# Channel-mix weights: f64 words loaded into their parts' room and converted there, 3 of 17 blocks in stage 1

## The chip, the cores and the metric

One NeuronCore of a Trainium2 chip runs the whole kernel. The metric is device time in microseconds (us) of one execution. The engines are called TensorE (PE in the profile, PEld for its weight loads), VectorE (DVE), ScalarE (ACT), GpSimd (POOL) and SyncE (SP, which here only issues DMAs).

## What is computed

Batch 4, 768 tokens, width 384. Three layers follow one another.

```python
# A: RWKV-like recurrence, 8 heads of 48
y[t] = r[t] @ (state + (u*k[t]) v[t]);  state = w[t]*state + k[t] v[t]
# B: 4 single-head causal attentions of width 64, each token gated to 2 of them
a = softmax(scale * (x wq[e]) (x wk[e])^T);  x = sum of gate * (a (x wv[e]) wo[e])
# C: channel mix, x_prev is x one token earlier
xk = mu_k*x + (1-mu_k)*x_prev;  xr = mu_r*x + (1-mu_r)*x_prev
out = sigmoid(xr @ w_r) * (maximum(xk @ w_k, 0)**2 @ w_v)
```

`w_k` (384x1024), `w_v` (1024x384) and `w_r` (384x384) of C arrive as float64, all else as float32. The products of B and C go through float32r in two parts: a number is a rounded high part and the rest, the low part, and three matmuls (high by high, low by high, high by low) stand for one.

## The kernel before

**Stages.** Stage 1 runs A for all batches, with B woven in as a second stream, and a third stream for the f64 conversion. It ends when A has ended: the pool `pA`, which holds A's tiles, is closed at line 1055. Stage 2 (lines 1068 to 1086) runs the rest of B with C for the first three batches, which goes over nine units of 256 tokens (`c_thin`, line 936). The end (`c_wide`, line 964) is C for the last batch in two units of 384 tokens.

**Order.** `run_all` (line 88) takes the next piece from the stream with the least progress, so the text order of A, B and C is fixed by costs written into the streams. A piece that yields nothing is put aside until another stream has moved. A scheduler of the language then orders each engine's instructions by that order and by its own model of when operands are ready.

**A, per pair of heads** (`a_prep`, `a_kt`, `a_u`, `a_pair`, 16 pairs): transposes, two long scans (lines 220 and 246) and products on VectorE, small matmuls on TensorE, a masking on GpSimd (line 338). Loads of the next pair go through SyncE's queue.

**B, per batch** (`phase_b`, line 575): values, gating, two projections of q and k (`proj`, line 544), 24 score blocks with a softmax, transposes (`trans`), products with the values (`av`) and with `wo` (`wo_half`, which stores x2 to DRAM through ScalarE's queue). In `trans` the transposed block goes from PSUM to SBUF on ScalarE (line 694), or on VectorE (line 692) for the blocks that `AT_DVE` (batches below `AT_B`) or `AT_DVE2` names; these are all 512 columns wide. In `proj` k's high part is written by ScalarE for one half of the partitions (line 142) and copied to the other half by a DMA of SyncE's queue (line 571).

**The conversion** (`c_convert`, `split_block`, lines 788 to 826): 34 blocks, 12 of `ck` (256 columns), 6 of `cr` and 16 of `cv` (192 columns), 7296 columns in all. Each is loaded through SyncE's queue into `c_raw` (two buffers). ScalarE scales the upper word (line 802), VectorE does three integer operations (803 to 805), ScalarE rounds to the high part (807), GpSimd subtracts for the low part (808), and two DMAs store both to DRAM. The integer operations use c_w1, written c_w in the rows.

**The weights in stage 2** (`c_weights`, line 828): six loads of GpSimd's queue bring both parts from DRAM into the pool `pW`, which lies where `pA` was, so the first waits for the end of A.

**C, per unit**: `c_load` brings x2 with one token ahead; `c_mix` forms xk (index 0) and xr (index 1); `c_hidden` makes eight blocks of 128 hidden columns (m = 0 to 7), `c_out` the gate `pz` from `cr` and the output `pvo` from `cv`. Within `c_hidden` the mix of xr goes along as a side stream, in `c_out` the next unit's mix of xk.

## Time and profile before

| what | value |
|---|---|
| median of 3 runs | 726.49 us (726.14 to 726.61) |
| profiled execution, its own time | 727.12 us |
| its span in the trace | 725.4 us |
| PE busy, share of the span | 672.8 us, 93% |
| PEld busy | 585.4 us, 81% |
| DVE busy | 497.9 us, 69% |
| ACT busy | 409.2 us, 56% |
| POOL busy | 299.7 us, 41% |
| moved by DMA | 77.88 MB |

Busy shares are means over the stages. Stage 1 lasts to about 325 us, stage 2 to about 640 us, the end to 725 us. The conversion's instructions stand between 66 and 248 us. A matmul's end is modelled, so busy PE is not PE at its peak. The profiled execution lies 1.7 us over its span and 0.6 us over the median of the runs.

### The profile page before, as it was taken

How to read it: one execution, taken by the hardware profiler on the slowest of the kernel's cores; microseconds unless marked ns; L12 is line 12 of the kernel's file. 1: busy time of each engine (PE TensorE's matmuls, PEld its weight loads, DVE VectorE, ACT ScalarE, POOL GpSimd, SP SyncE). 2: the span in 40 equal slices, each digit the busy share in tenths (PEclk: the TensorE clock that was granted, in tenths of full speed). 3: DMA queues.
4: the chain of work that ended last, by engine and by line, in shares of the span. 5: the costliest groups of instructions: out<-in, count | busy, mean ns of one | idle time of the engine just before them, and what ended most of it. 6: DMA issues, size and time to landing. Idle time of an engine off the chain costs nothing.

```text
span 725.4 us, 13681 instructions
## 1 busy us (share of the span) xinstructions
PE 672.8 (93%) x4938; PEld 585.4 (81%) x4938; DVE 497.9 (69%) x938; ACT 409.2 (56%) x1117; POOL 299.7 (41%) x397
## 2 busy tenths in 40 slices
PE   5887978889799999997999999999999999999995
PEld 4776856676577786866999899889898888989995
DVE  8988899998999888754543756556457573729520
ACT  3554556666576566656735657465556656534530
POOL 5876444343445222204625435362343515352320
PEclk9999899999999999999999999999999999999999
DMA  8797666668677653159320103211101101220001
GB/s 157 152 184 173 176 180 175 170 174 251 148 198 186 170 126 83 33 187 411 100 67 11 45 12 99 98 34 44 55 34 44 23 13 34 86 68 23 12 23 38
DMA packets 144205, 77.88 MB, mean 107 GB/s; under 512 B 109824, under 2 KB 138752, under 8 KB 143616
## 3 DMA queue, kind: packets, MB, share of 16 engines
q1 hardware_dynamic: 139936, 64.73, 35.1%
q0 software_dynamic: 864, 7.47, 2.6%
q10 hardware_dynamic: 3328, 4.72, 1.8%
q8 instruction: 41, 0.67, 0.4%
q14 instruction: 36, 0.29, 0.1%
HBM read 47.40 MB, written 23.99 MB: 98 GB/s over the span
## 4 chain that ended last, share of the span: by engine, by line
PE 64%; DVE 18%; DMA 8%; issue 4%; ACT 3%; POOL 1%; SPq 1%; ACTq 0%; DVEq 0%; POOLq 0%
PE ph L871 14%; PE pvo L871 14%; PE pz L871 5%; PE pa L710 5%; PE pq L518 4%; PE pt L681 3%; PE po L518 3%; PE py L368 3%; PE pv L518 3%; DMA c_raw<-in_moe_w_v_dram 2%; DVE ex L246 2%; PE psc L624 2%; PE pg L329 2%; DVE suf L220 2%; DVE rt L255 2%
## 5 line engine op out<-in xcount | busy, mean ns | idle before, releaser
L633 DVE TENSOR_REDUCE st<-psc 128x1 f32<-128x384 f32 (+4 forms) x128 | 62.1, 499 | 56.4 <-PE psc L629 41.3
L891 POOL TENSOR_TENSOR rl<-rl 128x256 f32<-128x256 f32 (+1 forms) x88 | 59.3, 678 | 78.5 <-ACT rl L890 78.3
L865 POOL TENSOR_TENSOR ml<-m,mh 128x256 fp32r<-128x256 f32 x54 | 40.6, 751 | 108.5 <-ACT mh L864 97.4
L645 ACT ACTIVATE A<-psc,st 128x384 f32<-128x384 f32 (+4 forms) x128 | 68.8, 542 | 20.2 <-DVE st L642 13.3
L871 PE MATMUL ph<-mh,ckh 128*128 128x256 f32 (+1 forms) x264 | 78.8, 299 | 0.9 <-ACT m L858 0.8
L871 PE MATMUL ph<-mh,ckl 128*128 128x256 f32 (+1 forms) x264 | 76.9, 292 | 1.5 <-DMA ckl<-ck_l_scratch 1.5
L338 POOL TENSOR_SCALAR_AFFINE_SELECT at<-at 128x512 f32<-128x512 f32 x48 | 44.7, 932 | 79.2 <-ACT at L337 79.0
L871 PE MATMUL ph<-ml,ckh 128*128 128x256 f32 (+1 forms) x264 | 76.9, 294 | 0.0
L871 PE MATMUL pvo<-cvh,hh 128*128 128x384 f32 x192 | 65.5, 341 | 0.0
L329 PE MATMUL pg<-rt,kt 128*128 128x256 f32 x192 | 53.8, 407 | 12.3 <-DVE um L307 5.8
L894 POOL TENSOR_TENSOR hl<-rl,hh 128x256 fp32r<-128x256 f32 x72 | 53.8, 756 | 27.0 <-ACT hh L892 26.7
L871 PE MATMUL pvo<-cvl,hh 128*128 128x384 f32 x192 | 64.6, 336 | 0.0
L871 PE MATMUL pvo<-cvh,hl 128*128 128x384 f32 x192 | 64.0, 336 | 0.0
L681 PE MATMUL pt<-ident,A 128*128 128x128 f32 x336 | 57.7, 275 | 0.0
L624 PE MATMUL psc<-k,q 128*128 128x384 f32 (+4 forms) x128 | 49.0, 383 | 9.0 <-ACT A L645 6.2
L890 ACT ACTIVATE rl<-ph 128x256 f32<-128x256 f32 (+1 forms) x88 | 35.5, 405 | 37.6 <-PE ph L871 26.2
L871 PEld LDWEIGHTS ph<-mh,ckh 128*128 128x128 f32 x264 | 49.9, 189 | 3.3 <-ACT m L858 1.0
L710 PE MATMUL pa<-at,vs 128*64 128x384 f32 (+2 forms) x288 | 52.1, 425 | 0.5 <-ACT at L694 0.5
L871 PEld LDWEIGHTS ph<-mh,ckl 128*128 128x128 f32 x264 | 50.0, 190 | 1.8 <-DMA ckl<-ck_l_scratch 1.8
L871 PEld LDWEIGHTS ph<-ml,ckh 128*128 128x128 f32 x264 | 49.9, 190 | 1.5 <-issue 1.5
L329 PEld LDWEIGHTS pg<-rt,kt 128*128 128x128 f32 x192 | 34.4, 197 | 19.8 <-DVE um L307 6.8
L861 DVE SCALAR_TENSOR_TENSOR m<-x2c,mu,m 128x256 f32<-128x256 f32 (+1 forms) x66 | 35.2, 539 | 20.4 <-ACT m L858 15.8
(172 smaller groups left out, 1917.3 us busy)
## 6 DMA issues: line engine op xcount, KB each, us to landing
x_scratch<-xs SPq DMA_DIRECT2D x24, 288.0 KB, 4.0
x<-x_scratch SPq DMA_DIRECT2D x6, 1152.0 KB, 8.4
nw<-in_w_dram SPq DMA_DIRECT2D x32, 144.0 KB, 3.7
nk<-in_k_dram SPq DMA_DIRECT2D x32, 144.0 KB, 3.1
nr<-in_r_dram SPq DMA_DIRECT2D x32, 144.0 KB, 2.8
nv<-in_v_dram SPq DMA_DIRECT2D x16, 288.0 KB, 3.2
out_dram<-rg SPq DMA_DIRECT2D x24, 192.0 KB, 1.9
c_raw<-in_moe_w_k_dram SPq DMA_DIRECT2D x12, 256.0 KB, 3.3
```

The source lines that it names most:

```text
L329: nc.tensor.matmul(pg[:, x * 2 * C : (x + 1) * 2 * C], lhsT=kt[:, c * C : (c + 1) * C], rhs=rt[:, c].rearrange("p h x -> p (h x)"), start= ...
L338: nc.gpsimd.affine_select(out=av, in_=av, pattern=[[0, 4], [1, C]], compare_op=OP.is_gt, fill=0.0, base=0, channel_multiplier=-1)
L518: nc.tensor.matmul(out, lhsT=a, rhs=c, start=i == 0, stop=i == n - 1)
L624: nc.tensor.matmul(o, lhsT=qs[e][:, tsl], rhs=ks[e][:, s0:s1], start=True, stop=False, skip_group_check=True)
L633: nc.vector.tensor_reduce(out=st[:, si : si + 1], in_=o, axis=AX.X, op=OP.max, negate=True)
L645: nc.scalar.activation(out=A[:, s0:s1], in_=p[:, 0 : s1 - s0], func=AF.Exp, bias=nm, accum_out=st[:, 3 + si : 4 + si])
L681: nc.tensor.transpose(pt[:, (j - j0) * 128 : (j - j0 + 1) * 128], A[:, j * 128 : (j + 1) * 128], ident)
L710: nc.tensor.matmul(pa[64 * e : 64 * e + 64, t0:HALF], lhsT=vs[:, j, 2 * pr + e], rhs=at[e][:, c0 : c0 + HALF - t0], start=j == 0, stop=j = ...
L865: eng.tensor_tensor(out=lo[:, j], in0=m1, in1=hi[:, j].bitcast(F32), op=OP.subtract)
L871: nc.tensor.matmul(out, lhsT=a, rhs=c, start=i == 0, stop=i == n - 1)
L891: nc.gpsimd.tensor_tensor(out=rl_, in0=rl_, in1=rl_, op=OP.mult)
L894: eng.tensor_tensor(out=hl[:, m], in0=rl_, in1=hh[:, m].bitcast(F32), op=OP.subtract)
```

## The change

The conversion no longer goes through DRAM. A block's f64 words are loaded by GpSimd's queue into the room that later holds its two parts, an intermediate word is made in another room, and the parts are written over the words. There are 17 blocks: 6 of `ck` (512 columns), 3 of `cr` and 8 of `cv` (384 columns). The first three of `ck` (`CW[:KT]`, hidden blocks m = 0 to 3) are loaded into the pool `const` early in stage 1 and converted halfway through A's stream, one after another, with `c_raw`'s two buffers as room. The other 14 are loaded when `pW` opens and converted in `c_thin` as a side stream of the first unit's `c_hidden`: after its blocks m = 0 to 6 come 1, 1, 1, 2, 2, 2 and 5 of them, and then the mix of xr, whose tiles (`mh1`, `ml1`) are the room until then. No other unit has a changed side stream.

The first token tile of C is loaded in stage 1, after batch 0 of B is done, and its mix of xk stands ahead of the weights' conversion. All tiles of x2 for `c_thin` now lie in `const`. k's other half is copied by ScalarE out of PSUM for batches 1 to 3, by DMA still for batch 0. `AT_DVE` is empty and `AT_B` is 1: batch 0 has no block copy on VectorE (before: two per pair and head), batches 1 to 3 have three (before: batch 1 two). The branch for other inputs, which does not run here, is changed alike.

```diff
-DUP = "dma"
-AT_DVE = ((5, 0), (4, 0))
+AT_DVE = ()
-AT_B = 2
+AT_B = 1
...
-                        if DUP == "act":
+                        if b:
-                        elif DUP == "pool":
-                            nc.gpsimd.tensor_copy(ks[e][oth, sl], ks[e][own, sl])
...
     NF = FF // 128
+    TN = 256
+    CW = tuple(
+        [("ck", w_k, j, 512 * g, (4, 2, 128)) for g in range(2) for j in range(KT)]
+        + [("cr", w_r, j, 0, (1, 2, DM)) for j in range(KT)]
+        + [("cv", w_v, j, 0, (1, 2, DM)) for j in range(NF)]
+    )
+    def c_weight_loads(pW, cw):
+        raws = []
+        for nm, src, j, o, (m, x, n) in cw:
+            words = 2 if src.dtype == I64 else 1
+            t = pW.tile([128, words * m * n], U32, tag=f"{nm}{j}_{o}", name="cw", bufs=1, padded_shape=[128, 2 * m * n])
+            nc.gpsimd.dma_start(t, src[j * 128 : (j + 1) * 128, o : o + m * n].bitcast(U32))
+            raws.append(t)
+        return raws
+    def c_rooms(pool, tags=("mh1", "ml1")):
+        return [
+            pool.tile([128, KT, TN], F32R, tag=t, name="cvs", bufs=1).rearrange("p k n -> p (k n)").bitcast(U32) for t in tags
+        ]
+    def c_convert(pW, cw, raws, room):
         V = nc.vector
+        for i, ((nm, src, j, o, (m, x, n)), raw) in enumerate(zip(cw, raws)):
+            w1 = room[i % 2][:, 0 : m * n]
+            w1f = w1.bitcast(F32)
+            if src.dtype != I64:
+                nc.scalar.copy(w1f, raw.bitcast(F32))
+            else:
+                wd = raw.rearrange("p (n two) -> p two n", two=2)
+                wlo, whi = wd[:, 0], wd[:, 1]
+                nc.scalar.activation(out=w1f, in_=whi.bitcast(F32), func=AF.Copy, scale=2.0 ** -112)
+                V.tensor_scalar(out=w1, in0=w1, scalar1=3, scalar2=None, op0=OP.logical_shift_left)
+                V.scalar_tensor_tensor(out=w1, in0=whi, scalar=0x80000000, in1=w1, op0=OP.bitwise_and, op1=OP.bitwise_or)
+                V.scalar_tensor_tensor(out=w1, in0=wlo, scalar=29, in1=w1, op0=OP.logical_shift_right, op1=OP.bitwise_or)
+            t = pW.tile([128, m, x, n], F32R, tag=f"{nm}{j}_{o}", name="cp", bufs=1)
+            v = w1f.rearrange("p (m n) -> p m n", n=n)
+            nc.scalar.copy(t[:, :, 0], v)
+            nc.gpsimd.tensor_tensor(out=t[:, :, 1], in0=v, in1=t[:, :, 0].bitcast(F32), op=OP.subtract)
+            wsp[nm, j, o] = t
+            yield 0
     mu = const.tile([128, 2, KT], F32, name="mu")
     om = const.tile([128, 2, KT], F32, name="om")
+    def c_load(pool, b, t0, n, bufs, q=nc.sync):
         t = pool.tile([128, KT, n + 1], F32, tag="x2c", name="x2c", bufs=bufs)
         if t0 == 0:
             nc.gpsimd.memset(t[:, :, 0:1], 0.0)
+            q.dma_start(t[:, :, 1 : n + 1], x2d[b, :, :, 0:n])
         else:
+            q.dma_start(t, x2d[b, :, :, t0 - 1 : t0 + n])
         return t
     def c_mix(pool, t, i, n, bufs, res):
...
-    def c_thin(pool, pst, units, n):
+    early = {}
+    def c_thin(pW, pool, pst, units, n):
-            mixes[u] = [c_load(pool, *units[u], n, 1), {}]
+            mixes[u] = [c_load(const, *units[u], n, 1), {}]
+        mixes[0] = [early.pop("x2c") if early else c_load(const, *units[0], n, 1, nc.gpsimd), {}]
+        conv = c_convert(pW, CW[KT:], c_weight_loads(pW, CW[KT:]), c_rooms(pool))
+        for _ in mix(0, 0):
+            pass
...
-            yield from c_side(c_hidden(pool, pst, mixes[u][1][0], n, 1, hs), mix(u, 1), 2)
+            if u == 0:
+                side = (list(next_n(conv, i)) for i in (1, 1, 1, 2, 2, 2, 5))
+                side = (c for g in (side, mix(u, 1)) for c in g)
+                yield from c_side(c_hidden(pool, pst, mixes[u][1][0], n, 1, hs), side, 1)
+            else:
+                yield from c_side(c_hidden(pool, pst, mixes[u][1][0], n, 1, hs), mix(u, 1), 2)
...
+    first = c_weight_loads(const, CW[:KT])
+    def x_stream():
+        while not bdone["n"]:
+            yield None
+        early["x2c"] = c_load(const, 0, 0, TN, 1)
+        yield 1
-    conv = stream(c_convert(), nconv * CV)
-    run_all(sB, sA, conv, until=sA)
-    for _ in conv[0]:
+    room = [pA.tile([128, 512], U32, tag="c_raw", name="cvs", bufs=CB) for _ in range(2)]
+    sK = stream(c_convert(const, CW[:KT], first, room), KT)
+    sK[2] = 0.5 * KT
+    run_all(sB, sA, sK, stream(x_stream(), 1), until=sA)
+    for _ in sK[0]:
...
-        c_weights(pW)
-        thin = c_thin(pC, psum_of(psC, {x: ("c", 2) for x in "hzo"}), thin_units, TN)
+        thin = c_thin(pW, pC, psum_of(psC, {x: ("c", 2) for x in "hzo"}), thin_units, TN)
```

## Rows read from the trace of the kernel before

**Rows 1.** Windows: stretch, then busy us (count) per engine, granted clock, DMA share, GB/s

```profile
60.00:250.00 190.00, 165.05 (x1361) 130.99 (x1359) 173.29 (x343) 116.93 (x321) 83.47 (x90) 0.96 0.70 182
200.00:240.00 40.00, 37.75 (x307) 29.93 (x305) 38.43 (x75) 26.22 (x72) 18.32 (x22) 1.00 0.71 185
250.00:325.00 75.00, 71.60 (x623) 57.97 (x622) 56.12 (x122) 45.05 (x126) 15.41 (x20) 1.00 0.45 115
325.00:366.00 41.00, 36.79 (x240) 31.99 (x239) 23.24 (x44) 27.69 (x76) 21.16 (x33) 1.00 0.61 226
340.00:361.00 21.00, 21.00 (x145) 18.64 (x144) 11.45 (x23) 17.27 (x49) 14.68 (x21) 1.00 0.49 172
366.00:640.00 274.00, 274.00 (x1857) 249.01 (x1856) 154.51 (x297) 158.63 (x457) 113.08 (x168) 1.00 0.15 46
```

**Rows 2.** Waits of 60 to 250 us, VectorE's longest: total us, times, longest

```profile
DVE c_w L803 <- ACT c_w L802: 3.6, 7, 1.6
```

**Rows 3.** Waits of TensorE from 340 us to the end, all there are

```profile
PE pz L871 <- ACT rl L890: 0.3, 1, 0.3
```

**Rows 4.** Timeline of TensorE: start us, duration us, instruction

```profile
343.62 0.28 PE L871 MATMUL ph<-mh,ckl 128*128 128x256 f32 x1
343.74 0.28 PE L871 MATMUL ph<-ml,ckh 128*128 128x256 f32 x1
```

**Rows 5.** Groups by line, VectorE, 0 to 335 us, the conversion: busy us, mean ns | idle before

```profile
L805 DVE SCALAR_TENSOR_TENSOR c_w<-c_raw,c_w 128x192 uint32<-128x192 uint32 (+1 forms) x34 | 18.2, 542 | 0.4
...
L804 DVE SCALAR_TENSOR_TENSOR c_w<-c_raw,c_w 128x192 uint32<-128x192 uint32 (+1 forms) x34 | 13.5, 406 | 0.3
...
L803 DVE TENSOR_SCALAR c_w<-c_w 128x192 uint32<-128x192 uint32 (+1 forms) x34 | 10.4, 310 | 3.8 <-ACT c_w L802 3.6
```

**Rows 6.** Groups of 60 to 250 us, the conversion on ScalarE

```profile
L802 ACT ACTIVATE c_w<-c_raw 128x192 f32<-128x192 f32 (+1 forms) x34 | 13.7, 402 | 12.0 <-DMA c_raw<-in_moe_w_v_dram 6.9 <-DMA c_raw<-in_moe_w_k_dram 2.6 <-DMA c_raw<-in_moe_w_r_dram 1.9
L807 ACT CAST c_hi<-c_w 128x192 fp32r<-128x192 f32 (+1 forms) x34 | 12.5, 374 | 13.2 <-DVE c_w L805 13.1
```

**Rows 7.** Groups by shape over the whole span: operations of 384 and 512 columns, and copies

```profile
L692 DVE COPY at<-pt 128x512 f32<-128x512 f32 x40 | 27.4, 685 | 9.8 <-PE pt L681 9.2
...
L633 DVE TENSOR_REDUCE st<-psc 128x1 f32<-128x512 f32 x16 | 11.0, 687 | 11.4 <-PE psc L629 11.3
...
L143 DVE TENSOR_TENSOR avl<-y,avh 128x384 fp32r<-128x384 f32 x16 | 9.7, 606 | 4.9 <-ACT avh L142 4.9
...
L915 DVE TENSOR_SCALAR rg<-rg 128x384 f32<-128x384 f32 x18 | 7.0, 390 | 13.5 <-ACT rg L914 13.5
...
L337 ACT COPY at<-pg 128x512 f32<-128x512 f32 x48 | 27.9, 586 | 10.3 <-PE pg L329 9.7 <-POOL at L338 0.3
...
L142 ACT CAST k<-pq 64x384 fp32r<-64x384 f32 x32 | 15.1, 473 | 8.3 <-DVE kl L143 5.7 <-PE pq L518 2.2
...
L461 POOL TENSOR_TENSOR wol<-st,woh 128x384 fp32r<-128x384 f32 x2 | 2.0, 1006 | 0.9 <-ACT woh L460 0.9
```

**Rows 8.** Timeline of GpSimd: first and last of the six weight loads

```profile
325.50 0.73 POOL L833 DMA_DIRECT2D ckh<-ck_h_scratch  x1 [14.92 <-PE pt L681]
...
328.30 0.59 POOL L833 DMA_DIRECT2D cvl<-cv_l_scratch  x1
```

**Rows 9.** DMA issues of 325 to 360 us: KB each, median us to landing

```profile
ckh<-ck_h_scratch POOLq DMA_DIRECT2D x1, 1536.0 KB, 7.2
...
cvl<-cv_l_scratch POOLq DMA_DIRECT2D x1, 1536.0 KB, 19.8
```

**Rows 10.** Timeline of TensorE: the wait for ckl, and the first pz

```profile
336.50 0.38 PE L871 MATMUL ph<-mh,ckl 128*128 128x256 f32 x1 [1.48 <-DMA ckl<-ck_l_scratch]
...
359.58 0.44 PE L871 MATMUL pz<-crh,mh 128*128 128x384 f32 x1
```

**Rows 11.** Instructions that read c_raw, one line of them: ns min/median/max, first and last start

```profile
L805 DVE SCALAR_TENSOR_TENSOR c_w<-c_raw,c_w x34: 335/410/1252, 68.0 to 246.6; 128x192 uint32<-128x192 uint32 x22, 128x256 uint32<-128x256 uint32 x12
```

**Rows 12.** DMA issues of the whole span: KB each, median us to landing

```profile
x_scratch<-x ACTq DMA_DIRECT2D x8, 384.0 KB, 2.7
```

More of the change, by code (lines that the diff above doesn't have):

```diff
@@ L43 @@
 XLO_POOL = range(0)
-CONV_DVE = 0
 M1_ACT = 3
@@ L778, in rwkv_moe_kernel @@
     NF = FF // 128
-    CW = (("ck", w_k, KT, FF), ("cr", w_r, KT, DM), ("cv", w_v, NF, DM))
-    csc = {
-        nm: [nc.dram_tensor(f"{nm}_{x}_scratch", (128, n0 * n1), F32R, kind="Internal").ap() for x in "hl"]
-        for nm, _, n0, n1 in CW
-    }
-    CQ_L, CQ_S = nc.sync, nc.sync
-    def split_block(src, hi, lo, n):
-        T = lambda tag, dt: pA.tile([128, n], dt, tag=tag, name=tag, bufs=CB, padded_shape=[128, 256])
-        if src.dtype != I64:
-            st = T("c_w1", F32)
-            nc.sync.dma_start(st, src)
-            nc.scalar.copy(hi, st)
-            nc.gpsimd.tensor_tensor(out=lo, in0=st, in1=hi.bitcast(F32), op=OP.subtract)
-            return
-        raw = pA.tile([128, 2 * n], U32, tag="c_raw", name="c_raw", bufs=CB, padded_shape=[128, 512])
-        CQ_L.dma_start(raw, src.bitcast(U32))
-        wd = raw.rearrange("p (n two) -> p two n", two=2)
-        wlo, whi = wd[:, 0], wd[:, 1]
-        w1 = T("c_w1", U32)
-        V = nc.vector
-        nc.scalar.activation(out=w1.bitcast(F32), in_=whi.bitcast(F32), func=AF.Copy, scale=2.0 ** -112)
-        V.tensor_scalar(out=w1, in0=w1, scalar1=3, scalar2=None, op0=OP.logical_shift_left)
-        V.scalar_tensor_tensor(out=w1, in0=whi, scalar=0x80000000, in1=w1, op0=OP.bitwise_and, op1=OP.bitwise_or)
-        V.scalar_tensor_tensor(out=w1, in0=wlo, scalar=29, in1=w1, op0=OP.logical_shift_right, op1=OP.bitwise_or)
-        w1f = w1.bitcast(F32)
-        nc.scalar.copy(hi, w1f)
-        (V if CONV_DVE else nc.gpsimd).tensor_tensor(out=lo, in0=w1f, in1=hi.bitcast(F32), op=OP.subtract)
@@ L828, in c_weights @@
-    def c_weights(pW):
-        for nm, src, n0, n1 in CW:
-            pr = []
-            for i, x in enumerate("hl"):
-                t = pW.tile([128, n0, n1], F32R, name=nm + x)
-                nc.gpsimd.dma_start(t.rearrange("p a b -> p (a b)"), csc[nm][i])
-                pr.append(t)
-            wsp[nm] = pr
+    TN = 256
[4 more added lines that the diff above has]
+    )
@@ L875, in c_hidden @@
     def c_hidden(pool, pst, mix, n, bufs, res):
-        ckh, ckl = wsp["ck"]
+        ck = lambda j, m, x: wsp["ck", j, 512 * (m // 4)][:, m % 4, x]
         kh, kl = mix
@@ L885, in c_hidden @@
                 ph[:, 0:n],
-                [t for j in range(KT) for t in ((ckh[:, j, ms], kh[:, j]), (ckl[:, j, ms], kh[:, j]), (ckh[:, j, ms], kl[:, j]))],
+                [t for j in range(KT) for t in ((ck(j, m, 0), kh[:, j]), (ck(j, m, 1), kh[:, j]), (ck(j, m, 0), kl[:, j]))],
             ):
@@ L906, in c_out @@
                 pz[:, 0:DM],
-                [t for j in range(KT) for t in ((rh[:, j, cs], crh[:, j]), (rh[:, j, cs], crl[:, j]), (rl[:, j, cs], crh[:, j]))],
+                [t for j in range(KT) for t in ((rh[:, j, cs], cr(j, 0)), (rh[:, j, cs], cr(j, 1)), (rl[:, j, cs], cr(j, 0)))],
             ):
@@ L918, in c_out @@
             pv = pst("o", "pvo")
-            terms = [t for m in range(NF) for t in ((hh[:, m, cs], cvh[:, m]), (hh[:, m, cs], cvl[:, m]), (hl[:, m, cs], cvh[:, m]))]
+            terms = [t for m in range(NF) for t in ((hh[:, m, cs], cv(m, 0)), (hh[:, m, cs], cv(m, 1)), (hl[:, m, cs], cv(m, 0)))]
             for k in mm_seq(pv[:, 0:DM], terms, 8):
@@ L1188, in rwkv_moe_kernel @@
         with ExitStack() as sg:
-            c_weights(sg.enter_context(tc.tile_pool(name="pW2", bufs=1, side="right")))
+            pW = sg.enter_context(tc.tile_pool(name="pW2", bufs=1, side="right"))
             pD = sg.enter_context(tc.tile_pool(name="pD2", bufs=1, side="left"))
+            for _ in c_convert(pW, CW, c_weight_loads(pW, CW), c_rooms(pD, ("cvs0", "cvs1"))):
+                pass
             psD = sg.enter_context(tc.tile_pool(name="psD2", bufs=1, space=PSUM))
```

28 lines of the change are left out of this document (2 added, 26 removed).

## The prediction

> **What bounds the kernel now.** I read the busy times by stretch first, then the waits, then the groups. From 60 to 250 us, the stretch that holds nearly the whole conversion, VectorE is busy 173.3 of 190 us, and its longest kind of wait adds up to 3.6 us, itself a part of the conversion [rows 1, 2]. So its queue nearly always holds ready work and VectorE bounds this stretch. From 250 to 325 us there is no conversion: VectorE falls to 56.1 of 75 us and TensorE takes over, its weight loads busy 58.0 of 75 us [rows 1]. From 366 to 640 us TensorE is busy all the time, its weight loads 91% of it, and from 340 us on all waits that the trace gives it come to 0.3 us [rows 1, 3]. There it is the bound, and work that is added elsewhere costs nothing until it makes TensorE wait. Just ahead of that lies a weak place: from 325 to 366 us TensorE is busy only 36.8 of 41 us, and it waits 1.48 us for ckl [rows 1, 10].
>
> TensorE's room is read from its weight loads rather than from its matmuls, since matmuls overlap: one that lasts 0.28 us starts 0.12 us after the one before it [rows 4].
>
> **Part 1: conversion taken from stage 1.** The three integer operations cost VectorE 10.4 + 13.5 + 18.2 = 42.1 us [rows 5]. ScalarE gives up 26.2 us of work, and 25.2 us in which it stood waiting for c_raw's DMAs or for VectorE ahead of these instructions [rows 6]; GpSimd gives up 34 subtractions. SyncE's queue loses 34 loads and 68 stores, so the loads of A's next pairs no longer stand behind them.
>
> Back come 3 blocks of 512 columns. No such operation is in the trace. From below I take 0.69 us (a reduction of 512 columns [rows 7]) for each two-operand one and 0.45 us for the shift (0.39 us at 384 columns [rows 7], a little more), 1.83 us a block; from above the old price by columns, 42.1 x 512 / 7296 = 2.95 us. The lower one rests on wide operations, so I take it: 5.5 us, at most 8.9. They come in one burst in the middle, and what A has queued behind them waits once for about that long; it is part of the sum. Their three load issues cost GpSimd about 0.6 us each [rows 8], beside the 31 subtractions that leave it for good.
>
> Batch 0's block copies go to ScalarE: 8 x 0.685 = 5.5 us off VectorE [rows 7], 8 x 0.586 = 4.7 us onto ScalarE, less than the 26.2 us that leave it. Batch 1 gets 4 more on VectorE, about half of them in stage 1: 1.4 us. VectorE's work falls by 42.1 - 5.5 + 5.5 - 1.4 = 40.7 us.
>
> How much of that is time? If VectorE stayed the bound, all of it: 41 us is the upper end. But TensorE then comes next. The stretch without conversion does 58.0 us of weight loads in 75 us. At this pace the 131.0 us of the stretch from 60 to 250 us take 131.0 x 75 / 58.0 = 169.5 us; scaled by its granted clock, 0.96 against 1.00 (1.00 is the upper level, 2.4 GHz, 0.96 a mixture with 1.2 GHz), 162.7 us [rows 1]. Half way is 166 us, a gain of **24 us**. VectorE would be busy 132.6 of 166 us, 80%, near its 75% in the stretch I took as the measure, so the pace is plausible. Lower end: the best pace reached with the conversion still there, 29.9 of 40 us from 200 to 240 us, gives 175 us and a gain of 15 us.
>
> Here a rule speaks for less. The Trainium skill ("Perfetto Trace Analysis", Identifying the Most-Contended Engine) says that the busy share of matmuls is no good measure of how near TensorE is to its limit, and to take that of the weight loads. The overlap in rows 4 agrees. By the matmuls the same working gives 165.1 x 75 / 71.6 = 172.9 us, a gain of 17 us and a time of 713.5 us; by the rule it is the 24 us above.
>
> **Part 2: conversion added to stage 2.** Fourteen blocks are loaded and converted between the end of A and the first unit's gate, whose first matmul now starts at 359.6 us [rows 10]. Loads: the six of before, 7296 KB, were issued from 325.5 us on and landed by 328.3 + 19.8 = 348.1 us [rows 8, 9]; 5760 KB at that rate need 18 us, to about 343 us, and the first three blocks, as many bytes as ckh, about 7 us. The loads are in time. They can't start earlier: the first waits for A's last tiles as ckh did (14.9 us idle on GpSimd ahead of it [rows 8]). Their 14 issues keep GpSimd for 8 us instead of 3.5, and the mix's subtraction for the first unit stands behind them.
>
> The work: VectorE needs 11 x (0.39 + 2 x 0.606) + 3 x 1.83 = 23.1 us; the 0.606 us is a 384-column operation with two SBUF operands [rows 7]. Its idle time from 325 to 366 us is 17.8 us [rows 1]: 5 us too little. ScalarE needs 11 x 2 x 0.473 + 3 x 2 x 0.586 = 13.9 us, with four copies of k 15.8 us [rows 7], against 13.3 us idle [rows 1]: 2.5 us too little. GpSimd needs 11 x 1.0 + 3 x 1.3 us (scaled by columns) and 4.5 us of issues, 19.4 us against 19.8 us idle [rows 1, 7]. So VectorE decides, and the conversion ends some 5 us late. The mix of xr, which has to wait for its rooms, adds 3 us ahead of the gate. TensorE can do part of B in these 8 us; I put its loss at 6 us. From below it is nothing, if the scheduler finds B's matmuls for all of it. From above it is 20 us: blocks going one after another, each with 0.47 + 1.60 + 0.47 us and, an estimate, 0.3 us between engines, 2.9 us, end at 330 + 14 x 2.9 = 371 us, the mix at 374 us, 14 us late, and 6 us for C's evacuations queued behind them on ScalarE.
>
> In return the first hidden blocks find their weights and their token tile in place. I take 2 us (the 1.48 us for ckl and a little of the start; none to 4). Net loss of part 2: **4 us** (-4 to 20).
>
> A rule here speaks against the change. The line-805 operations took from 0.335 to 1.252 us [rows 11]. The Trainium skill ("SBUF — State Buffer", Who interferes with whom) says that a VectorE instruction with two SBUF inputs and a GpSimd one that reads SBUF exclude each other, the second waiting for all of the first. The spread agrees. GpSimd is busy 70% of the time from 340 to 361 us against 44% in stage 1 [rows 1], so some 0.3 us more on each of 28 operations would be 8 us, a net loss of about 10 us, and 712.5 us in place of 706.5.
>
> **Part 3: the rest.** k's copies add 24 x 0.473 = 11.4 us to ScalarE [rows 7], mostly in stage 2, where it is busy 58% [rows 1], and take 24 DMAs off SyncE's queue. The score matmuls are queued behind them, but TensorE waits for nothing there [rows 3]; zero, between 3 us gained and 3 us lost. The early load of the token tile makes SyncE's queue wait for the last x2 stores of batch 0, 2.7 us to landing [rows 12]; behind it are loads for A's next pairs. Zero, at most 3 us. The end is untouched.
>
> **Sum.** Profiled execution 727.1 - 24 + 4 + 0 = 707.1 us; it lay 0.6 us over the median, so **706.5 us**.
>
> **The rivals.** (a) VectorE's whole 40.7 us becomes time, since ScalarE's waits go as well: 727.1 - 41 + 4 - 0.6 = 689.5 us. For it: ScalarE's 25 us of waits. Against: TensorE would need the weight-load share of 131 / 149 = 88%, which it only has in stage 2. (b) TensorE holds at the pace of 200 to 240 us, and stage 2 loses 10: 727.1 - 15 + 10 - 0.6 = 721.5 us. (c) Slower: the blocks crawl on ScalarE, where each instruction waits in order. From 340 to 361 us it is idle only 3.7 of 21 us [rows 1]; a block of 0.95 us at 18% takes 5.3 us, the fourteenth is ready at 404 us, the gate at 407 us, 47 us late. If TensorE loses half of that and k's copies cost 3 us, it is 727.1 - 24 + 27 - 0.6 = 729.5 us. It decides from about 4.9 us a block. Against it: B's own ScalarE work would be late with it. (d) The change moves no time: gain and loss cancel near 726 us.
>
> **How the numbers follow.** Forecast (698 to 716 us) 0.52; (a) 0.13; (b) 0.20; (c) 0.11; (d) 0.04. Up to 724 us the range leaves out (c) and (d), 0.15; down to 690 us it leaves out little of (a). Faster by over 0.2% (1.5 us, about what a measurement of this kernel can tell from no change) 0.85, within it 0.04, slower 0.11.
>
> **What would show it.** A has ended near 301 us instead of 325; VectorE's share up to there is near 80%, and the weight loads' near 77%. The c_raw waits are gone. In the 40 us after A, TensorE waits for cr, cv or the mix of xr by some 6 us, and later for nothing. It is wrong if stage 1 shortens by under 15 us, if the first gate comes more than 20 us later after A's end than now, or if waits for k's copies appear in stage 2.

## The result

The changed kernel takes 736.42 us (736.05 to 738.19) against 726.46 us (726.14 to 726.61) of the kernel before beside it: ratio 1.0143, 95% interval 1.0125 to 1.016. It is slower by 10 us (1.4%); the forecast was 20 us faster. The later sets were timed with the kernel before at 726.3 to 727.5 us (median by set), so each ratio below is taken within its own set, and a difference of two edits is given by the times and, where it matters, by the ratios.

| | before | after |
|---|---|---|
| span of the profiled execution, us | 725.4 | 734.5 |
| first weight load of stage 2, us from the start | 325.5 | 304.9 |
| first pz (the gate) after that load, us | 34.1 | 64.3 |
| from the gate to the end, us | 365.8 | 365.3 |
| mean granted clock of TensorE | 0.984 | 0.967 |

The table holds the account in outline; its lines of before are those of [rows 8, 10]. Stage 1 gave 20.6 us. Then the gate came 30.2 us later behind the first load than before, and from the gate on both kernels take about the same time. From the first load to the end the loss is 429.6 - 399.9 = 29.7 us.

The windows of the kernel after (stretch, busy us and count by engine, granted clock, DMA share, GB/s) answer to [rows 1]:

```profile
60.00:304.00 244.00, 231.06 (x2032) 190.76 (x2031) 200.24 (x369) 152.74 (x405) 78.49 (x81) 0.99 0.49 117
304.00:344.00 40.00, 30.21 (x161) 24.46 (x160) 27.25 (x53) 23.77 (x64) 23.55 (x32) 0.79 0.44 163
344.00:366.00 22.00, 15.97 (x84) 12.29 (x83) 21.28 (x32) 15.18 (x36) 14.91 (x16) 0.84 0.01 1
304.90:369.20 64.30, 49.08 (x265) 39.88 (x266) 48.95 (x86) 40.28 (x102) 40.16 (x49) 0.81 0.30 111
640.00:680.00 40.00, 36.81 (x227) 35.18 (x226) 36.55 (x49) 23.12 (x52) 25.64 (x27) 1.00 0.03 11
```

and the same stretch, first load to gate, of the kernel before:

```profile
325.50:359.60 34.10, 29.90 (x200) 25.38 (x200) 17.64 (x37) 25.05 (x71) 19.25 (x31) 1.00 0.71 266
```

TensorE made 200 matmuls in 34.1 us before and 265 in 64.3 us after; the 65 more were block B's. At the pace of before, 265 matmuls are 45.2 us: 19 us are lost here. From the first load to the end (before, then after) TensorE has the same work:

```profile
325.50:725.40 399.90, 387.94 (x2545) 357.58 (x2545) 215.82 (x404) 217.48 (x600) 155.60 (x229) 1.00 0.19 62
304.90:734.50 429.60, 401.84 (x2549) 364.67 (x2549) 252.83 (x452) 240.16 (x645) 182.99 (x250) 0.97 0.15 50
```

Of the 29.7 us, 15.8 are idle time of TensorE (12.0 before, 27.8 after) and 13.9 are matmuls that take longer. B's 65 matmuls made ahead of the gate brought next to nothing behind it: there TensorE is busy 5.3 us less than before (352.8 and 358.0 us), but idle 4.8 us more. Between 640 and 680 us it has waits that were not there before, with VectorE busy 36.55 of 40 us; B's last product is then done (its last po at 630 us, before at 644), and C is alone.

What TensorE waits for from 300 to 420 us, where from 340 us on [rows 3] had 0.3 us in all (total us, times, longest):

```profile
PE psc L620 <- ACT A L641: 7.5, 3, 3.8
PE po L516 <- ACT k L565: 4.0, 2, 2.4
```

Its timeline there (start, us, instruction, idle before):

```profile
308.35 0.34 PE L621 MATMUL psc<-kl,q 128*128 128x384 f32 x1
312.49 0.69 PE L620 MATMUL psc<-k,q 128*128 128x384 f32 x1 [3.81 <-ACT A L641]
...
316.16 0.80 PE L620 MATMUL psc<-k,q 128*128 128x512 f32 x1 [2.10 <-ACT A L641]
...
320.22 0.78 PE L856 MATMUL ph<-ml,cp 128*128 128x256 f32 x2
...
324.30 0.52 PE L516 MATMUL po<-avl,woh 128*128 128x384 f32 x1
...
328.34 0.34 PE L516 MATMUL po<-avl,woh 128*128 128x384 f32 x1
```

Three things are to be read here. Block B's softmax is late (the waits for A). The first hidden block's third product, which takes the mix's lo (ml), comes at 320.2 us, so C's work can't fill the gaps. And the clock is down after the first gap: the po matmul that takes 0.34 us at 328 us took 0.52 us at 324 us. The granted clock is at 0.50, the lower of its two levels (1.2 of 2.4 GHz), in these two stretches:

```profile
312.00:328.00 16.00, 10.75 (x36) 8.03 (x37) 9.00 (x18) 8.01 (x23) 6.17 (x10) 0.50 0.66 264
359.00:364.00 5.00, 3.69 (x10) 3.19 (x11) 4.90 (x8) 2.66 (x5) 2.68 (x3) 0.50 0.00 0
```

TensorE is busy 14.4 us in them. If half of that is the clock's, it is some 7 of the 13.9 us (an estimate). Ahead of the second stretch the hidden layer is done (its last product at 349.6 us), and B's po waits for evacuations that share ScalarE and VectorE with the conversion (the 4.0 us for k, and 1.3 us for VectorE).

ml is late because of GpSimd's queue. Its timeline, the answer to [rows 8]:

```profile
304.86 1.65 POOL L790 DMA_DIRECT2D cw<-in_moe_w_k_dram  x3 [8.94 <-PE pt L677]
...
311.54 0.54 POOL L790 DMA_DIRECT2D cw<-in_moe_w_v_dram  x1 [1.77 <-DMA cw<-in_moe_w_k_dram]
312.79 0.54 POOL L790 DMA_DIRECT2D cw<-in_moe_w_v_dram  x1 [0.71 <-DMA cw<-in_moe_w_k_dram]
...
316.27 0.75 POOL L850 TENSOR_TENSOR ml<-m,mh 128x256 fp32r<-128x256 f32 x1
```

The 14 issues take 11.4 us, not 8: the last five each stand until an earlier load has landed. ScalarE stands for loads too, with the softmax behind it, and VectorE for ScalarE, with the softmax's statistics (st) behind that (ScalarE, then VectorE):

```profile
308.53 0.66 ACT L811 ACTIVATE cvs<-cw 128x512 f32<-128x512 f32 x1 [2.13 <-DMA cw<-in_moe_w_k_dram]
311.27 0.66 ACT L811 ACTIVATE cvs<-cw 128x512 f32<-128x512 f32 x1 [2.09 <-DMA cw<-in_moe_w_k_dram]
311.84 0.51 ACT L641 ACTIVATE A<-psc,st 128x320 f32<-128x320 f32 x1
```
```profile
309.22 0.43 DVE L812 TENSOR_SCALAR cvs<-cvs 128x512 uint32<-128x512 uint32 x1 [1.64 <-ACT cvs L811]
309.56 1.34 DVE L629 TENSOR_REDUCE st<-psc 128x1 f32<-128x320 f32 x3
```

And VectorE's part of the conversion, from 300 to 372 us (busy us, mean ns | idle before), against [rows 5, 7]:

```profile
L813 DVE SCALAR_TENSOR_TENSOR cvs<-cw,cvs 128x384 uint32<-128x384 uint32 (+1 forms) x14 | 13.0, 929 | 0.3
...
L814 DVE SCALAR_TENSOR_TENSOR cvs<-cw,cvs 128x384 uint32<-128x384 uint32 (+1 forms) x14 | 10.7, 767 | 0.2
...
L812 DVE TENSOR_SCALAR cvs<-cvs 128x384 uint32<-128x384 uint32 (+1 forms) x14 | 6.4, 458 | 2.5 <-ACT cvs L811 2.4
```

30.1 us where 23.1 were forecast, and VectorE is busy 21.28 of 22 us from 344 to 366 us.

The suspects have the numbers that the expectations use: VectorE's work (theory 1); ScalarE's queue, where the early mix and the operations that stand for raw words are ahead of the softmax (theory 2); k's copies on ScalarE (theory 3). The transpose copies were undone without a number of their own. GpSimd's queue (theory 5) was only taken up after the first four runs; no expectation names a theory 4.

### The profile page after: what moved, and what is told of

Same layout as the page of the kernel before. It is cut to its first block, busy times and chain, and to the rows that moved or that the text cites. A ratio compares the mean times of both kernels' runs of the same rounds, so it can differ in the third digit from the quotient of the medians.

```text
span 734.5 us, 13284 instructions
## 1 busy us (share of the span) xinstructions
PE 678.6 (92%) x4938; PEld 591.2 (80%) x4938; DVE 498.6 (68%) x883; ACT 420.5 (57%) x1113; POOL 303.0 (41%) x391
## 4 chain that ended last, share of the span: by engine, by line
PE 63%; DVE 21%; ACT 6%; DMA 5%; issue 3%; SPq 1%; POOL 1%; DVEq 0%; ACTq 0%; POOLq 0%
PE pvo L856 11%; PE ph L856 10%; PE pa L706 6%; PE py L366 4%; PE pz L856 4%; PE pq L516 4%; PE po L516 4%; PE pt L677 4%; PE pg L327 3%; PE psc L620 3%; PE pv L516 3%; DVE suf L218 3%; PE ptr L199 3%; PE psc L621 2%; DMA x2c<-x_scratch 2%
## 5 line engine op out<-in xcount | busy, mean ns | idle before, releaser
L856 PE MATMUL ph<-mh,cp 128*128 128x256 f32 (+1 forms) x528 | 107.7, 299 | 3.9 <-ACT rl L874 3.5
L856 PE MATMUL pvo<-cp,hh 128*128 128x384 f32 x384 | 99.5, 338 | 0.0
L856 PEld LDWEIGHTS ph<-mh,cp 128*128 128x128 f32 x528 | 84.9, 190 | 8.6 <-ACT rl L874 5.5
L856 PE MATMUL ph<-ml,cp 128*128 128x256 f32 (+1 forms) x264 | 76.8, 294 | 0.0
L856 PEld LDWEIGHTS pvo<-cp,hh 128*128 128x128 f32 x384 | 69.0, 188 | 1.2 <-ACT A L641 0.6
L856 PE MATMUL pvo<-cp,hl 128*128 128x384 f32 x192 | 64.9, 338 | 0.1
L856 PEld LDWEIGHTS ph<-ml,cp 128*128 128x128 f32 x264 | 50.0, 190 | 0.0
L849 ACT CAST mh<-m 128x256 fp32r<-128x256 f32 (+1 forms) x66 | 28.0, 427 | 34.5 <-DVE m L846 29.8
L876 ACT CAST hh<-rl 128x256 fp32r<-128x256 f32 (+1 forms) x88 | 37.4, 427 | 15.9 <-POOL rl L875 15.1
L900 DVE RECIPROCAL rg<-rg 128x384 f32<-128x384 f32 x18 | 45.9, 2549 | 0.4
```

Of the source, the lines that this page charges most:

```text
L856: nc.tensor.matmul(out, lhsT=a, rhs=c, start=i == 0, stop=i == n - 1)
L900: nc.vector.reciprocal(out=rg, in_=rg)
```

## The experiments

**The integer operations left out.** The 14 blocks of stage 2 keep their loads, scaling, rounding and subtraction, but not the three integer operations, so these weights are never converted.

```diff
-    def c_convert(pW, cw, raws, room):
+    def c_convert(pW, cw, raws, room, ints=True):
...
+                if ints:
+                    V.tensor_scalar(out=w1, in0=w1, scalar1=3, ...)
...
-        conv = c_convert(pW, CW[KT:], c_weight_loads(pW, CW[KT:]), c_rooms(pool))
+        conv = c_convert(pW, CW[KT:], c_weight_loads(pW, CW[KT:]), c_rooms(pool), False)
```

> The changed kernel, but the 14 blocks converted after A leave out the three integer operations on VectorE (30.1 us of VectorE there in the changed kernel); loads, ScalarE's and GpSimd's steps stay. So what these weights hold is meaningless. Theory 1 (VectorE's conversion after A starves TensorE, about 20 us of the 30 us lost there): 716 us or less, and the granted clock after A back near 1.00. Theory 2 (ScalarE's queue: the early mix and the instructions that wait for the f64 loads stand ahead of the softmax): 733 us or more, the waits of 3.8, 2.1 and 1.6 us for the softmax remain. Theory 3 (k's copies on ScalarE): 735 us.

723.62 us, ratio 0.9934 [0.9907, 0.9961]. 12.8 us less than the changed kernel by the times, 15 by the ratios, in between the two expectations: VectorE's work is a good part of the loss, not all of it. The clock didn't come back as theory 1 had it (0.83 from the first load to the gate), and TensorE's waits for the softmax stayed as theory 2 had it (7.8 us).

**The small parts, undone one at a time.** k's copies by DMA again; the token tile loaded in stage 2; the transpose copies back on VectorE.

```diff
-                        if b:
-                            nc.scalar.copy(ks[e][oth, sl], src)
-                        else:
+                        if True:
                             nc.sync.dma_start(ks[e][oth, sl]..., ks[e][own, sl]...)
```
```diff
-        mixes[0] = [early.pop("x2c") if early else c_load(..., nc.gpsimd), {}]
+        mixes[0] = [early.pop("x2c") if early else c_load(const, *units[0], n, 1), {}]
...
-        early["x2c"] = c_load(const, 0, 0, TN, 1)
```
```diff
-AT_DVE = ()
-AT_B = 1
+AT_DVE = ((5, 0), (4, 0))
+AT_B = 2
```

> The changed kernel with k's other half copied by DMA for all batches, as before. Theory 3 (k's copies on ScalarE delay the scores and the evacuations after A): 728 us or less. Theories 1 and 2: 735 to 737 us, since only four copies fall into the 75 us in which the time is lost.

> The changed kernel without the early token tile: the first tile is loaded by SyncE's queue where C begins, as before; the mix still stands ahead of the conversion. Theory 2 (the mix is in ScalarE's queue before its room is free and holds up the softmax, 3.6 us, then an idle TensorE at a lower clock): 728 us or less, and no wait of ScalarE for a DMA of xs. Theory 1: 735 to 739 us, the mix is a little later and the conversion as before.

> The changed kernel with the block copies of batches 0 and 1 placed as before: batch 0 two on VectorE, batch 1 two instead of three. If the copies' move has a part in the loss (batch 1's extra copy of 0.69 us falls into the stretch after A, where VectorE is busy 19.4 of 20 us): 733 us or less. Else 735 to 740 us, stage 1 up to 4 us longer by 5.5 us more of VectorE.

739.62 us (1.0159 [1.0124, 1.0194]), 737.72 us (1.0129 [1.0095, 1.0163]) and 741.30 us (1.0178 [1.0137, 1.022]). None of the three makes the kernel faster, so none is the loss. With the transpose copies back on VectorE the first load comes at 315.6 us instead of 304.9: that part is worth 10.8 us in stage 1, and 4.9 us at the end (2.5 by the ratios). k's copies by ScalarE are worth 3.2 us (1.2 by the ratios). At the end neither is clear of the noise: the intervals overlap that of the changed kernel.

**The loads on SyncE.**

```diff
-            nc.gpsimd.dma_start(t, src[j * 128 : (j + 1) * 128, o : o + m * n].bitcast(U32))
+            nc.sync.dma_start(t, src[j * 128 : (j + 1) * 128, o : o + m * n].bitcast(U32))
```

> The changed kernel with the 14 raw-word loads of the second stage issued by SyncE in place of GpSimd; all else as it is. In the changed kernel the first load starts at 304.86 us, the fourteenth at 316.26, the last five each behind the landing of an earlier one, and the lo of the first mix follows only at 316.27 although its hi was ready at 305.7; TensorE's hidden-layer group waits for it to 320.22. Theory 5 (part of the loss is GpSimd's queue: the loads hold up the mix, and the idle time lets TensorE's clock fall): the lo then ends near 307, TensorE's stop of 308.7 to 320 shrinks to some 4 us, and the time is 722 to 729 us. Theory 1 alone (the loss is the conversion's VectorE and GpSimd work itself, 30.1 us of VectorE in an engine that is 95% busy): the mix comes sooner, the converted blocks come no sooner, and the time stays at 734 to 738. If SyncE's other transfers (the scratch reads of block A) queue behind the 14 loads, ScalarE's wait of 3.64 us for one of them grows and the time is 738 or more.

724.89 us (722.9 to 727.17), ratio 0.9979 [0.9954, 1.0004]: 11.5 us less than the changed kernel, level with the kernel before. ml and the third product come 11 to 12 us sooner (GpSimd's timeline, then TensorE's):

```profile
305.68 0.73 POOL L850 TENSOR_TENSOR ml<-m,mh 128x256 fp32r<-128x256 f32 x1 [9.71 <-ACT mh L849]
```
```profile
308.41 0.40 PE L856 MATMUL ph<-ml,cp 128*128 128x256 f32 x2
```

**Both edits.**

> The changed kernel with both edits: the 14 loads issued by SyncE, and the 14 blocks of stage 2 without their three integer operations on VectorE (these weights are left unconverted, so the output means nothing). Alone the first edit took 11.5 us off, the second 12.8. If the two are separate causes (a queue ahead of the mix, and VectorE's work), they add: 711 to 714 us. If they are one cause seen twice (VectorE's work only hurts because everything starts late, or the other way round), the pair gives little over the better one: 719 to 723 us.

713.6 us (712.87 to 714.94), ratio 0.9836 [0.9803, 0.987]. Most of it adds: 22.8 us less than the changed kernel, where 11.5 and 12.8 make 24.3. Time in us, and in brackets the span from the first load to the end in the profiled execution (before: 399.9; the 415.8 is of an execution 3 us under its median):

| | loads by GpSimd | loads by SyncE |
|---|---|---|
| with the integer operations | 736.4 (429.6) | 724.9 (419.8) |
| without them | 723.6 (415.8) | 713.6 (408.2) |

Of the 29.7 us, 9.8 hang on who issues the loads and 11.6 more on the integer operations (in the other order 7.6 and 13.8); 8.3 us stay even without both. These two windows of the kernel with both edits show TensorE with little idle time soon after the first load:

```profile
304.00:344.00 40.00, 35.62 (x221) 28.18 (x221) 20.94 (x40) 35.58 (x95) 28.39 (x35) 0.96 0.44 163
344.00:380.00 36.00, 36.00 (x256) 34.96 (x255) 21.83 (x49) 22.59 (x67) 16.23 (x25) 1.00 0.16 51
```

**What is it in GpSimd's loads?** First, the mix written ahead of the loads in the program:

```diff
-        conv = c_convert(pW, CW[KT:], c_weight_loads(...), c_rooms(pool))
         for _ in mix(0, 0):
             pass
+        conv = c_convert(pW, CW[KT:], c_weight_loads(...), c_rooms(pool))
```

> The changed kernel with the first mix's three subtractions put ahead of the 14 loads in GpSimd's queue; the loads stay on GpSimd. It tells which half of theory 5 is right. If the loss is the mix standing behind the issues: the gain is that of the loads on SyncE, 723 to 728 us. If what SyncE gained is that the loads themselves come earlier and are issued by a queue on which nothing waits, the loads now start 7 to 10 us later (the third subtraction ended at 316 us with SyncE's loads, and GpSimd can issue only behind it), the conversion ends later, and the time is 733 to 740 us.

736.93 us (1.0146 [1.01, 1.0191]). Neither theory was put to the test: the planner that orders each engine's work by its own modelled times put the loads ahead again (first load at 306.3 us, ml at 317.9). Next, nine loads on GpSimd and the last five on SyncE:

```diff
-            nc.gpsimd.dma_start(t, ...)
+            (nc.gpsimd if i < 9 else nc.sync).dma_start(t, ...)
```

> The changed kernel with the first nine of stage 2's loads on GpSimd and the last five on SyncE. The order of the instructions on the engines stays nearly the changed kernel's (130 lines of difference on TensorE, where all 14 loads on SyncE made 1879), but the five issues that stood 3.8 us on GpSimd behind the landing of earlier loads are gone from its queue. So it parts two things that the run with all loads on SyncE mixed. If the queue itself is the loss: the first mix's lo ends near 311 us in place of 317, TensorE's stop ends some 5 us sooner, and the time is 728 to 731 us. If the 11.5 us came from another order of the instructions: the order is kept here, and the time is 734 to 738 us.

734.4 us (1.0101 [1.0054, 1.0148]). Only 2 us, in the range that stood for another order of the instructions. But it did not free the queue as meant, so it decides nothing. SyncE's five loads now ran first, the two loads that are needed first landed later, and the wait moved: one issue stood 2.95 us on GpSimd, so that ml came at 312.9 us, and ScalarE stood with the softmax behind it:

```profile
312.11 0.66 ACT L811 ACTIVATE cvs<-cw 128x512 f32<-128x512 f32 x1 [5.43 <-DMA cw<-in_moe_w_k_dram]
312.68 0.52 ACT L641 ACTIVATE A<-psc,st 128x320 f32<-128x320 f32 x1
```

Then ScalarE was taken out of it, its scaling given to GpSimd, with the loads on GpSimd and on SyncE:

```diff
-                nc.scalar.activation(out=w1f, in_=whi.bitcast(F32), func=AF.Copy, scale=2.0 ** -112)
+                if len(cw) == len(CW) - KT:
+                    nc.gpsimd.tensor_scalar(out=w1f, in0=whi.bitcast(F32), scalar1=2.0 ** -112, ...)
+                else:
+                    nc.scalar.activation(out=w1f, in_=whi.bitcast(F32), func=AF.Copy, scale=2.0 ** -112)
```

> The changed kernel with the conversion's first operation, the scaling of the high words, on GpSimd in place of ScalarE for the 14 blocks of stage 2; the loads stay on GpSimd. In the changed kernel ScalarE stood 2.13 and 2.09 us at this operation for a load to land, in the run with nine and five loads 5.43 us, each time with block B's softmax behind it; TensorE waited for the softmax 7.5 and 6.6 us and its clock fell. If ScalarE's queue, held up by the loads, is what the order of the instructions turns on: the softmax no longer waits, TensorE's waits for it fall under 3 us, and the time is 722 to 729 us. If it is GpSimd's and VectorE's work alone: GpSimd gets 14 more operations of about 1 us beside 14 issues and 14 subtractions, the conversion ends later, and the time is 735 to 742 us.

> The same with all 14 loads on SyncE, so that neither GpSimd nor ScalarE stands for a load ahead of other work. If both queues count: 716 to 722 us, clearly below both kernels. If the loads on SyncE already gave what there is: 723 to 727. If GpSimd's 14 operations more delay the subtractions, or make VectorE's two-operand operations longer (mean 0.77 and 0.91 us with SyncE's loads) by the rule of exclusion: 728 or more.

735.37 us (1.012 [1.0085, 1.0155]) and 730.27 us (1.0047 [1.0025, 1.0069]). The theory that ScalarE's waits for loads are the cause fell in the form in which it could be tried: these waits are off ScalarE, but TensorE's waits for the softmax grow to 11.2 us, ScalarE's for VectorE's softmax statistics ahead of it come to 12.9, and GpSimd pays 19 us. The gate is worth a look here: with GpSimd's loads it comes at 383.0 us, 14 us later than in the changed kernel, and the end still 1 us sooner. How late the gate is doesn't alone say how long the kernel takes. The waits of the kernel with GpSimd's loads (first line TensorE's, then ScalarE's), and one group of GpSimd:

```profile
PE psc L620 <- ACT A L641: 11.2, 9, 1.9
...
ACT A L641 <- DVE st L638: 7.2, 4, 3.0
...
ACT A L641 <- DVE st L629: 5.7, 6, 2.2
```
```profile
L812 POOL TENSOR_SCALAR cvs<-cw 128x384 f32<-128x384 f32 x11 | 14.3, 1298 | 0.4
```

Last, the loads left on GpSimd, and only the first mix's three lo subtractions taken out from behind them:

```diff
-            eng.tensor_tensor(out=lo[:, j], in0=m1, in1=hi[:, j].bitcast(F32), op=OP.subtract)
+            (nc.vector if lo_v else eng).tensor_tensor(out=lo[:, j], ...)
```

> The changed kernel, loads on GpSimd, with the three lo subtractions of the first token tile's first mix on VectorE in place of GpSimd, so that they don't stand behind the 14 issues. In the six runs with the loads on GpSimd the first hidden block's third product came 14 us or more after the first load (in the changed kernel at 320.2 us, the hidden layer's later blocks from 333 us on), in the four with all loads on SyncE about 4 us after it (at 308 us, later blocks from 320). If this late start of the hidden layer, the work that TensorE would have had while block B's softmax was late, is the cause: the third product comes near 308 us, the later blocks near 320, and the time is 724 to 729 us. If it only goes along with something else that SyncE's loads bring (their landing, the issues' own 8 us on GpSimd ahead of the conversion's subtractions): 733 to 738 us.

728.08 us (725.65 to 730.54), ratio 1.0024 [1.0004, 1.0043]: 8.3 us less than the changed kernel. The issues stand on GpSimd as before, but ml doesn't, and the third product comes 12 us sooner (GpSimd, VectorE, TensorE):

```profile
311.05 0.54 POOL L790 DMA_DIRECT2D cw<-in_moe_w_v_dram  x1 [1.79 <-DMA cw<-in_moe_w_k_dram]
```
```profile
305.32 0.43 DVE L850 TENSOR_TENSOR ml<-m,mh 128x256 fp32r<-128x256 f32 x1
```
```profile
308.10 0.40 PE L856 MATMUL ph<-ml,cp 128*128 128x256 f32 x2
```

So about 8 of the 11.5 us go with the hidden layer's late start behind the issues. In the trace (421.3 us from the first load to the end, 8.3 less) 3 us of it are TensorE's idle time and 5 us shorter matmuls: the granted clock from the first load to the gate is 0.94, where it was 0.81. The edit also changes the planner's order, so it isn't shown that the size is the queue's alone.

**The conversion's other costs, with the loads on SyncE.** The 14 subtractions moved to VectorE, and the first tile's multiplication moved from ScalarE to GpSimd:

```diff
-            nc.gpsimd.tensor_tensor(out=t[:, :, 1], in0=v, ...)
+            (nc.vector if len(cw) > KT else nc.gpsimd).tensor_tensor(out=t[:, :, 1], in0=v, ...)
```
```diff
-            if (M1_ACT >> i) & 1 and bufs == 1:
+            if m1_act and (M1_ACT >> i) & 1 and bufs == 1:
...
+            return c_mix(pool, mixes[u][0], i, n, 1, mixes[u][1], u > 0)
```

> The changed kernel with the loads on SyncE and the 14 subtractions of the conversion on VectorE in place of GpSimd. By the rule of exclusion the conversion's second and third integer operations (mean 0.93 and 0.77 us, in two heaps near 0.54 and 1.25) lose their long heap and fall to some 0.55 to 0.6 us: 14 x 0.55 us less, 14 subtractions of 0.55 more, so VectorE's sum stays near 30 us and the time at 722 to 728, no worse than with GpSimd. If the long heap has another cause, the operations stay long, VectorE has 8 us more, and the time is 729 to 734 us.

> The changed kernel with the loads on SyncE and, for the first token tile alone, the mix's first multiplication on GpSimd in place of ScalarE. With SyncE's loads ScalarE still stood 3.5 us at this multiplication for a store out of the tile that had its room, with the evacuation of block A's output behind it, and 2.9 us for GpSimd. If these waits of ScalarE are what TensorE's 6.0 us of waits for the softmax come from: 2 to 5 us less, 720 to 723. If TensorE is late for VectorE in any case: 724 to 727. If six more GpSimd operations beside the conversion delay it: above 728.

The first: 727.2 us (1.0018 [1.0003, 1.0033]), 2.3 us more than with GpSimd, in the range of the rule that the expectation names, though no gain. The groups with the loads on SyncE, first with GpSimd's subtractions, then with VectorE's:

```profile
L814 DVE SCALAR_TENSOR_TENSOR cvs<-cw,cvs 128x384 uint32<-128x384 uint32 x11 | 10.0, 913 | 0.2
L813 DVE SCALAR_TENSOR_TENSOR cvs<-cw,cvs 128x384 uint32<-128x384 uint32 x11 | 8.4, 766 | 0.3
```
```profile
L813 DVE SCALAR_TENSOR_TENSOR cvs<-cw,cvs 128x384 uint32<-128x384 uint32 x11 | 7.1, 645 | 0.2
L814 DVE SCALAR_TENSOR_TENSOR cvs<-cw,cvs 128x384 uint32<-128x384 uint32 x11 | 7.0, 640 | 0.1
```

The same operations fall by a sixth to a third once GpSimd isn't at work on the blocks, so the slower ones are GpSimd's doing. The second: 726.15 us (0.9995 [0.9978, 1.0011]), no gain. TensorE's waits for the softmax fell from 6.0 to 3.9 us, but it now waits 4.2 us for mh instead of 2.4.

**The kernel before, improved in place.** Wide blocks in stage 1; the small parts alone; both.

```diff
-            n = 256 if n1 % 256 == 0 else n1 // 2
+            n = 512 if n1 % 512 == 0 else n1
...
-        w1 = T("c_w1", U32)
+        w1 = lo.bitcast(U32)
```

> The kernel before with its conversion in 17 wide blocks (512 or 384 columns) in place of 42 narrow ones; the first word's room is shared with lo, and the way through DRAM is kept. It tells whether the narrow blocks' fixed cost is what stage 1 can be rid of without moving work to stage 2. Conversion on VectorE in stage 1 falls by estimate from 42.1 us to some 27. By the measured gain of the changed kernel (40.7 us of VectorE work taken away, first load of stage 2 20.6 us earlier) 15 us taken away should bring 6 to 8 us: 718 to 721. If TensorE's own pace binds stage 1 by then the gain is nearer 3 us (723). If the end of stage 1 hangs on the conversion's last blocks, it is 726 or more.

> The kernel before with the change's two small parts alone: the transpose copies that VectorE had given to ScalarE as in the changed kernel, and k's copy by ScalarE in the second batch. Undoing the first in the changed kernel cost 4.9 us, undoing the second 3.2 us. If they are worth the same where the conversion stays in stage 1: 718 to 722. If they are only worth it beside a conversion in stage 2: 725 to 728. If ScalarE takes on more than it can in stage 1: above 728.

> The kernel before with the wide blocks and both small parts. If the gains add: 711 to 716. If they compete for the same VectorE idle time of stage 1, so that TensorE binds after the first: 716 to 721, no better than the better of the two alone.

730.07 us (1.0047 [1.0025, 1.0068]), 727.11 us (1.0009 [0.999, 1.0028]) and 725.98 us (0.9991 [0.9967, 1.0015]). No gains to add. With 17 wide blocks in place of 34 (the expectation's 42 is a slip) VectorE's conversion took 37.2 us instead of the 27 expected: the three operations of a 384-column block are only a tenth cheaper by the column than those of 192 (2.15 us against 1.20), and the second is dearer, 886 ns here against 362 ns (x22) at 192 columns:

```profile
L804 DVE SCALAR_TENSOR_TENSOR c_lo<-c_raw,c_lo 128x384 uint32<-128x384 uint32 x11 | 9.7, 886 | 0.1
```

The first load stayed where it was, at 327.0 us. With the small parts as well it came at 320.6 us, 4.9 us sooner than in the kernel before, and stage 2 gave that back.

**Half and half.** ck and cr through stage 1 and DRAM as before, the 8 blocks of cv in stage 2 with SyncE's loads; then the same with the small parts.

```diff
-    CW = (("ck", ...), ("cr", ...), ("cv", w_v, NF, DM))
+    CW = (("ck", ...), ("cr", ...))
+    CV_B = [("cv", w_v, j, 0, (1, 2, DM)) for j in range(NF)]
...
+        conv = c_convert_late(pW, CV_B, c_weight_loads(pW, CV_B), c_rooms(pool))
```

> Half and half: ck and cr converted in stage 1 in narrow blocks and sent through DRAM as in the kernel before (9 of 17 blocks, 58% of the columns), the 8 blocks of cv loaded by SyncE as raw words and converted in stage 2 as in the changed kernel; copies as before. If both stages' losses are proportional to the columns, stage 1 gains 0.42 x 20.6 = 8.7 us and stage 2 loses 8/14 of the 20 us that the run with SyncE's loads lost: 11, the time is 727 to 731. If both stages take some conversion into their idle time and lose steeply only beyond it: 717 to 723, below both kernels.

> The half-and-half kernel with the change's small parts, the transpose copies and k's copy on ScalarE. In the changed kernel they were worth 4.9 and 3.2 us, in the kernel before nothing (727.1 against 726.6). If they pay where VectorE is relieved in stage 1: 3 to 6 us below the half-and-half kernel. If they pay only where the whole conversion has left stage 1: the same as it within 1.5 us.

728.55 us (1.002 [0.9998, 1.0042]) and 739.52 us (1.0161 [1.0116, 1.0205]). The first lies where losses in proportion to the columns put it, though both terms are larger: stage 1 gives 11.2 us (the first load at 314.3 us) where 8.7 were expected, and stage 2 takes 14.6, not 11. This one point in the middle is no better than the ends. The small parts, worth at most 5 us each in the changed kernel and nothing in the one before, cost 11 us here; why isn't shown. ScalarE stands longer for raw words (6.9 us against 5.1), TensorE longer for the softmax (10.7 us against 5.2), and the granted clock from 320 to 340 us is 0.66 against 0.80 (a wait of TensorE, one of ScalarE, and a window of the kernel with the small parts):

```profile
PE psc L624 <- ACT A L645: 10.7, 3, 6.5
...
ACT cvs L867 <- DMA cw<-in_moe_w_v_dram: 6.9, 4, 2.9
```
```profile
320.00:340.00 20.00, 11.36 (x49) 9.26 (x49) 12.78 (x29) 10.10 (x27) 4.35 (x5) 0.66 0.95 359
```

No version that converts all its weights beats the kernel before beyond its uncertainty; the nearest is the changed kernel with SyncE's loads.

## Why the prediction was wrong

- **Part 1 was right in size** (24 us, 15 to 41): stage 1 ended 20.6 us sooner, and from 60 to 304 us VectorE was busy 82% and the weight loads 78%, where 80 and 77 were forecast. The weight loads' pace gave 24 and the matmuls' 17; the measured value lies in the middle and favours neither. That VectorE's sum alone sets it isn't shown: 4.9 us less of it (the wide blocks) moved the first load of the kernel before by nothing, and 4.1 us more (the transpose copies, 5.5 less 1.4) moved the changed one's by 10.8 us.
- **Part 2 failed**, in its "Net loss of part 2", put at 4 us (-4 to 20); the loss is 29.7 us. Three terms of it:
  - "The mix's subtraction for the first unit stands behind them." The wait was named and given no price. Taking it away gave 8.3 us: it held up the hidden layer, the work that TensorE would have had while B's softmax was late. "Their 14 issues keep GpSimd for 8 us" was short as well: 11.4 us.
  - The conversion's 23.1 us on VectorE were 30.1, and leaving them out gave 12.8 us. The measure, 0.606 us [rows 7], came from other stretches; here the 384-column operations took 0.97 and 0.79 us on average. The section "Who interferes with whom" of "SBUF — State Buffer" (the Trainium skill) states that a VectorE instruction with two SBUF inputs contends with a GpSimd one that reads SBUF. The trace agrees (0.91 and 0.77 us fall to 0.64 without GpSimd's subtractions), and the prediction's estimate by it, 8 us more, is close to the 7 us more that came. By itself it gave 712.5 us, so it was right and didn't decide.
  - "TensorE can do part of B in these 8 us; I put its loss at 6 us." The gate came 30.2 us later, not 8. TensorE did do part of B, but lost 15.8 us idle and 13.9 us in longer matmuls. It waited for B's own chain (softmax 7.5 us, k 4.0 us), not for cr, cv or the mix of xr, and the clock, at 0.50 for 16 us and for 5 us, is a term that part 2 doesn't have.
- **Part 3 held in time**: k's copies lie within their bounds, and the early tile costs nothing that can be told (737.72 us without it). But waits for k's copies, one of the prediction's own signs of being wrong, did appear (4.0 us). With the copies by DMA again, TensorE waits 2.9 us for kl in the same place, so they aren't the copies' alone.
- **The rivals.** The sign was in (c), at 729.5 us with a chance of 0.11, and its size was near: it put the fourteenth block 78 us behind the first load and the gate 47 us late; measured are 63 and 30 us. The way was another: it took ScalarE's order as the limit, but from 344 to 366 us VectorE is the busy one (21.28 of 22 us; ScalarE 15.18), and TensorE lost nearly all of the delay, not half. GpSimd's queue has no price in (c) either. And no rival joined the named waits: each was set against the idle time of its own engine, while TensorE stood idle with the softmax and ml late at once.
- **Left open.** 8.3 us of the loss remain without the integer operations and with SyncE's loads. And the planner's order changes with every edit: the small parts gave +11 us in the half-and-half kernel. A difference of a few us between two variants here is no proof of its cause unless the trace shows the wait.

## What to carry to other kernels

Price every wait that you name, with whoever stands behind it: a burst of loads on an engine that also computes the first input of the next stage delays that stage's start by as long as the burst stands (here 11 us, and 8 us of the kernel's time). When work moves out of a stage bound by one engine into one with idle time, ask which instruction ends the gate there and what TensorE has to do until then; idle shares by engine don't add up to a place for a chain that goes from ScalarE to VectorE, back to ScalarE and on to GpSimd. Where a planner sets the order, check in the trace that the order asked for is the one that ran.
